# Half of the inner units at a time for the first two token blocks, with weight conversion at half the pace

## The chip, the cores and the metric

The kernel runs on one core of a Trainium2 chip. The metric is the device time of one execution in microseconds (us). Engines are called as the profile calls them: PE is TensorE's matmul, PEld its weight load, DVE is VectorE, ACT is ScalarE, POOL is GpSimd, and SP is SyncE, whose queue starts most DMAs.

## The reference

Three stages follow each other: a windowed attention, a routed mixture of eight experts, and a dense feed-forward with a squared ReLU. Only the last one is changed:

```python
def _moe2_ref(x, w_in, w_out):            # x [2176, 512], w_in [512, 2048], w_out [2048, 512]
    h = np.maximum(x @ w_in, 0.0)
    return (h * h @ w_out).astype(np.float32)
```

[...]

## The kernel before

**Precision.** Each matmul operand is split into a "high" float32r part and the "low" rest (`copy_hi` on ACT, line 65; `sub_lo` on DVE, line 68; `sub_lo_pool` on POOL, line 71), and each product is three matmuls: high by high, low by high, high by low.

**Token blocks and inner units.** The 17 tiles of 128 tokens make five blocks of 4, 4, 3, 3 and 3 tiles. The 2048 inner columns make 16 inner units of 128 (`FC2 = 16`), counted by `fc`. One *step* is `ff1(i, fc)` and then `ff2` of the step before. `ff1` runs 12 matmuls (lines 1105 to 1107) into a PSUM tile `fh`, ACT does Relu, Square and the high part (`ahi`), DVE the low part (`alo`). `ff2` runs 3 matmuls for each token tile (lines 1125 to 1127) and adds into PSUM tiles `fo` that stay open through all 16 steps of a block; only line 1127 reads `alo`. There are four `fo` buffers. After the 16th unit, `fo` is copied to an `os` tile (even token tiles on ACT, line 1133; odd ones on DVE, line 1131) and stored by a DMA of SP (line 1135).

**Inputs of a block.** `y_load` fetches a tile of the experts' output `yd` into `yin` (line 1082), `y_tile` transposes it on PE into `ytr` (line 1090) and splits it (`yhi`, `ylo`). `yin` and `os` share three buffers of the tag `io`.

**Weights.** The 32 weight units, 16 of `w_in` and 16 of `w_out` in turn, are loaded (`conv_load`, 512 KB each, three buffers), turned into float32 (`conv_value`: one instruction on ACT, line 717, five on DVE, lines 718 to 722) and split (`conv_split`: ACT, then POOL). A *tick* `k` of `conv` splits unit k - 2, converts unit k and starts the load of unit k + 2. All units then stay in SBUF. The first ten ticks lie among the experts (`on_take`, from chunk `CFROM = 12` on, one every `CSTEP = 5` chunks, at most `2 * NFE + 2` of them); the other 24 lie in the first block's steps, `RATE / 4` = 1.75 a step.

**Order.** Everything stands under a manual schedule: each engine, SP's queue too, runs its instructions in the order in which the program states them, and waits for what the next one needs.

Of the kernel before, what the change touches and what calls it, by code (L numbers as in the profile page):

```python
# [10 lines left out]
F32 = mybir.dt.float32  # L11
# [4 lines left out]
ALU = mybir.AluOpType  # L16
# [5 lines left out]
P = 128  # L22
NEG = -8e9
EXTRA = 3
# [5 lines left out]
def tile_attention_moe_ffn(  # L30
# [16 lines left out]
    nc = tc.nc  # L47
    B, H, S, D = q_l.shape
    SG = q_g.shape[2]
    NE, DM, FF = w1.shape  # L50
    FF2 = w_in.shape[1]
    ST = S + SG
    NTOK = B * ST
# [4 lines left out]
    FC2 = FF2 // P  # L58
# [16 lines left out]

    xd = dr.tile([NTOK, DM], F32, name="xd")
    yd = dr.tile([NTOK, DM], F32, name="yd")

# [1 line left out]
    ident = cp.tile([P, P], F32, name="ident")  # L80
    make_identity(nc, ident)
    mask = cp.tile([P, 3, KW], F32, name="mask")
# [10 lines left out]
    ths = cp.tile([P, MAXOV, NE], F32, name="ths")  # L93
    jrow = cp.tile([P, MAXOV], F32, name="jrow")

    # routing state
    rank = cp.tile([P, NTILE], F32, name="rank")
    ohs = cp.tile([P, NTILE, NE], BF16, name="ohs")
    val = cp.tile([P, NTILE, 4], F32R, name="val")
# [48 lines left out]
        g.memset(slot, 0.0)  # L148
        g.memset(ohsum, 0.0)

# [1 line left out]
    early = ctx.enter_context(ExitStack())  # L152
    wp = early.enter_context(tc.tile_pool(name="wp", bufs=1))
    LEADV = 5
    NRAW, NHL = 8, 6
    LOOK = NHL - 2
    NFE = 4
    RATE = 7
    CSTEP = 5
    CFROM = 12  # L160
    n_split = [0]

    def load_chunk(kind, p, c):
        """four rows of 128 of w1, or as many pairs of row blocks of w2"""
        raw = wp.tile([P, 1024], F32, tag="raw", bufs=NRAW, name="raw")
        e = pass_expert[p]
        w = w1 if kind == 1 else w2
        src = w[e:e + 1] if isinstance(e, int) else w[ds(e, 1)]
        if kind == 1:
            nc.sync.dma_start(out=raw, in_=src[:, c * P:(c + 1) * P, :].rearrange("o p f -> p (o f)"))  # L170
        else:
            r = c * 2 * P
            nc.sync.dma_start(
                out=raw.rearrange("p (k d) -> p k d", k=2),
                in_=src[:, r:r + 2 * P, :].rearrange("o (k p) d -> p (o k) d", p=P),
            )
        return raw
# [8 lines left out]
            sub_lo(lo, raw, hi)  # L186
        return hi, lo

    # an expert per pass: the first and the last by number, the others in an order found on the chip
    NX = NE  # L190
    pass_expert = {0: 0, 1: NE - 1}
    segs = [(1, 0)]
# [33 lines left out]
        on_take(i)  # L226
        return chunks.pop((kind, p, c))

    # =================== attention ===================
    att = ctx.enter_context(ExitStack())  # L230
    ap_ = att.enter_context(tc.tile_pool(name="ap", bufs=1))
    ps = att.enter_context(tc.tile_pool(name="ps", bufs=1, space=PSUM))
# [238 lines left out]
    cur = [0]  # L471

    def route(c, x):
        """gate, expert, rank within the expert and slot of the 128 tokens of tile c"""
        z = {}

        def s1():
# [88 lines left out]
            later.append((i0 + d_, f_, c, n_))  # L566
        later.sort(key=lambda p: p[0])

    # order of the attention's units
    units = []  # L570
    for b in range(B):
        for t in range(NT):
# [35 lines left out]
    with tc.manual_schedule():  # L608
# [61 lines left out]
            do_later()  # L670
        dv(len(micro))

        # =================== slots of the experts ===================
        att.close()
        fe = ctx.enter_context(tc.tile_pool(name="fe", bufs=1, side="right", reuse_waits="tile"))
        cv = ctx.enter_context(tc.tile_pool(name="cv", bufs=1, side="right", reuse_waits="tile"))
# [2 lines left out]
        mps = mo.enter_context(tc.tile_pool(name="mps", bufs=1, space=PSUM, reuse_waits="tile"))  # L679
        NHS, NHH = 4, 4  # L680

# [1 line left out]
        wpool = [fe]  # L683
        wff = {}
        craw, cval = {}, {}
# [47 lines left out]
            wff[u] = (hi, lo)  # L733

        def conv(ticks):
            """the first steps of the conversion: unit k - 2 split, unit k's value, unit k + 2 loading"""
            while n_conv[0] < min(ticks, NU + 2):
                k = n_conv[0]
                if k >= 2:
                    conv_split(k - 2)  # L740
                if k < NU:
                    conv_value(k)
                if k + 2 < NU:
                    conv_load(k + 2)
                n_conv[0] += 1
# [1 line left out]
        conv_[0] = conv  # L747

        def slot_indices(ids_, n, nm):
            """token + 1 (0: empty) -> rows to gather (empty: row 0) and to scatter (empty: beyond)"""  # L750
            gi = mp.tile([P, n], I32, name="gi" + nm)
            si = mp.tile([P, n], I32, name="si" + nm)
            em = mp.tile([P, n], F32, name="em" + nm)
            nc.vector.tensor_scalar(out=gi, in0=ids_, scalar1=-1.0, scalar2=0.0, op0=ALU.add, op1=ALU.max)
            nc.vector.tensor_scalar(out=em, in0=ids_, scalar1=0.0, scalar2=8192.0, op0=ALU.is_equal, op1=ALU.mult)
            nc.vector.scalar_tensor_tensor(out=si, in0=ids_, scalar=-1.0, in1=em, op0=ALU.add, op1=ALU.add)
            return gi, si
# [20 lines left out]
        gather_pass(0)  # L778
        gather_pass(1)

        # the experts between the first and the last, those with more than 128 tokens first: the
        # first EXTRA passes take two tiles; the general path takes what is left
        ND = NE - 2
        dd = slice(1, 1 + ND)
        tot = mps.tile([P, 512], F32, tag="tr", bufs=2, name="tot")
# [22 lines left out]
        nc.vector.tensor_copy(eji[:, ND:ND + 1], c1[:, 0:1])  # L808

        def all_bases():  # L810
            """first key and expert of every tile beyond the first of an expert, level by level"""
            lev = mp.tile([P, 2, MAXOV], F32, name="lev")
            nc.vector.tensor_reduce(out=lev[:, 0, :], in_=ov, op=ALU.add, axis=AX.X)
            fl = mp.tile([P, MAXOV, NE], F32, name="fl")
# [20 lines left out]
            return kb, kbi  # L835

        def all_keys():
            """rank + 4096 * expert + 1 of every routed token, 0 of the others"""
            key = mp.tile([P, NTILE], F32, name="key")
            kw = mp.tile([P, NTILE, NE], F32, name="kw")  # L840
            nc.vector.tensor_tensor(out=kw, in0=ohs, in1=ecol.unsqueeze(1).to_broadcast([P, NTILE, NE]), op=ALU.mult)
            nc.vector.tensor_reduce(out=key, in_=kw, op=ALU.add, axis=AX.X)
            nc.vector.tensor_tensor(out=key, in0=key, in1=rank, op=ALU.add)
            return key

        def any_slots(base, key):
            """slots of the tile whose first key is base"""
            acc = mps.tile([P, 512], F32, tag="tr", bufs=2, name="acc")
            kr = mp.tile([P, NTILE], F32, tag="kr", bufs=1, name="kr")
            nc.vector.tensor_scalar(out=kr, in0=key, scalar1=base, scalar2=-1.0, op0=ALU.subtract, op1=ALU.add)  # L850
            for c in range(NTILE):
                mt = mp.tile([P, P], F32R, tag="mt2", bufs=2, name="mt2")
                nc.vector.tensor_scalar(out=mt, in0=iota[:, 0:P], scalar1=kr[:, c:c + 1], scalar2=None, op0=ALU.is_equal)
                nc.tensor.matmul(acc[:, 0:4], mt, val[:, c, :], start=(c == 0), stop=(c == NTILE - 1))
            sl = mp.tile([P, 4], F32, tag="sl", bufs=1, name="sl")
            nc.vector.tensor_copy(sl, acc[:, 0:4])
            nc.vector.tensor_tensor(out=sl[:, 1:2], in0=sl[:, 1:2], in1=sl[:, 2:3], op=ALU.add)
            g_, s_ = slot_indices(sl[:, 0:1], 1, "g")
            return g_, s_, sl[:, 1:2]

# [1 line left out]
        n_over = nc.values_load(eji[0:1, ND:ND + 1], min_val=0, max_val=MAXOV, skip_runtime_bounds_check_because="counted")  # L862
        with tc.If(n_over > 0):
            kb, kbi = all_bases()
# [41 lines left out]
                    bounds_check=NTOK - 1, oob_is_err=False,  # L906
                )

        # =================== experts ===================
        conv_load(0)  # L910
        conv_load(1)
        sel = mp.tile([P, ND, ND], F32, name="sel")
# [138 lines left out]
        mo.close()  # L1051
        early.close()

        # =================== squared-ReLU feed-forward ===================
        fp = ctx.enter_context(tc.tile_pool(name="fp", bufs=1, reuse_waits="tile"))
        fps = ctx.enter_context(tc.tile_pool(name="fps", bufs=1, space=PSUM))
        wpool[0] = fp
# [35 lines left out]
            copy_hi(hi[:, :, c], mv)  # L1093
            sub_lo(lo[:, :, c], mv, hi[:, :, c])

        acts, outs = {}, {}

        def ff1(i, fc):
            n = sizes[i] * P
# [14 lines left out]
            sub_lo(lo[:, 0:n], r[:, 0:n], hi[:, 0:n])  # L1114
            acts[i, fc] = (hi, lo)

        def ff2(i, fc):
            hi, lo = acts.pop((i, fc))
            whi, wlo = wff[2 * fc + 1]
            if fc == 0:  # L1120
                outs[i] = [fps.tile([P, 512], F32, tag="fo", bufs=4, name="fo") for _ in range(sizes[i])]
            for j in range(sizes[i]):
                c = slice(j * P, (j + 1) * P)
                o = outs[i][j]
                nc.tensor.matmul(o, hi[:, c], whi, start=(fc == 0), stop=False)  # L1125
                nc.tensor.matmul(o, hi[:, c], wlo, start=False, stop=False)  # L1126
                nc.tensor.matmul(o, lo[:, c], whi, start=False, stop=(fc == FC2 - 1))  # L1127
                if fc == FC2 - 1:
                    a = fp.tile([P, DM], F32, tag="io", bufs=3, name="os")
                    if j % 2:  # L1130
                        nc.vector.tensor_copy(a, o)
                    else:
                        nc.scalar.copy(a, o)
                    r0 = (starts[i] + j) * P
                    nc.sync.dma_start(out=out[r0:r0 + P, :], in_=a)

        y_block(0)
        for j in range(3):
# [3 lines left out]
            if j == 0:  # L1142
                y_load(0, 3)
        prev = None
        for i in range(nb):
            for fc in range(FC2):
                ff1(i, fc)
                if i == 0:
                    conv(2 * NFE + 2 + RATE * (2 * fc + 1) // 8)
                if prev is not None:  # L1150
                    ff2(*prev)
                prev = (i, fc)
                if FC2 - 7 <= fc < FC2 - 3:
                    y_load(i + 1, fc - FC2 + 7)
                if i == 0:
                    conv(2 * NFE + 2 + RATE * (fc + 1) // 4)
                if i + 1 < nb:
                    if fc == FC2 - 5:
                        y_block(i + 1)
                    if FC2 - 5 <= fc < FC2 - 5 + sizes[i + 1]:  # L1160
                        y_tile(i + 1, fc - FC2 + 5)
        ff2(*prev)


# [26 lines left out]
```

## Time and profile before

| What | Value |
|---|---|
| Timed runs | median 846.65 us of 3 (845.98 to 846.96) |
| The profiled execution's own time (its span, first to last instruction) | 847.4 us |
| PE busy | 773.1 us, 91% |
| DVE busy | 438.4 us, 52% |
| ACT busy | 405.0 us, 48% |
| POOL busy | 164.0 us, 19% |
| HBM read and written | 74.21 MB and 16.25 MB |
| First `ff1` matmul of block 0, of block 1, of block 2 | 438.30, 547.56, 636.77 us |

The span is that of one profiled execution, on the slowest (here the only) core. The page gives nothing outside the span. A busy share is an average over the whole span, so the stretch that the change touches is read by itself.

### The profile page before, as it was taken

Reading aid. Unit: us, or ns where it says so; the run is one execution under the profiler, and the core shown is the slowest. Engines: PE = TensorE matmul, PEld = TensorE weight load, DVE = VectorE, ACT = ScalarE, POOL = GpSimd, SP = SyncE. Lnnn points to the kernel's source line nnn. Section 1 sums busy time; section 2 is a strip of 40 time slices with the busy share of each in tenths; the row PEclk is TensorE's granted clock in tenths of the full one; section 3 lists DMA queues with packets and bytes.
Section 4 is the critical chain, followed back from the end, with each engine's and each line's share of the span. In section 5 each row is a group of like instructions: output and inputs, shape, how many; then the busy total and the mean of one; then the engine's idle time right before and its main releaser. Section 6 shows DMA issues by size and latency. Waiting matters only on the chain.

```text
span 847.4 us, 12121 instructions
## 1 busy us (share of the span) xinstructions
PE 773.1 (91%) x4337; PEld 673.3 (79%) x4337; DVE 438.4 (52%) x1103; ACT 405.0 (48%) x863; POOL 164.0 (19%) x169
## 2 busy tenths in 40 slices
PE   7999999999938978796869878999999999999998
PEld 6998989989836968585647666788889999999997
DVE  5667656665544898898819999411111121111111
ACT  5666646545305764758116556333343344344333
POOL 4013200000013564748204344100000000000000
PEclk9999999999858999899869999999999999999999
DMA  9868954331126877777123445020002002000001
GB/s 178 203 161 189 239 136 99 98 84 51 50 70 212 264 228 249 241 276 258 37 87 92 132 129 169 1 87 1 1 1 87 1 1 75 1 1 38 1 1 38
DMA packets 103071, 90.35 MB, mean 107 GB/s; under 512 B 70594, under 2 KB 78786, under 8 KB 103008
## 3 DMA queue, kind: packets, MB, share of 16 engines
q1 hardware_dynamic: 101248, 84.71, 34.7%
q0 software_dynamic: 1760, 4.84, 1.7%
q8 instruction: 35, 0.57, 0.3%
q14 instruction: 28, 0.23, 0.1%
HBM read 74.21 MB, written 16.25 MB: 107 GB/s over the span
## 4 chain that ended last, share of the span: by engine, by line
PE 38%; DVE 9%; issue 2%; DMA 1%; ACT 0%; SPq 0%; POOLq 0%
PE fo L1127 6%; PE fh L1105 6%; PE fo L1126 6%; PE fh L1106 6%; PE fh L1107 6%; PE fo L1125 6%; DVE tb L719 2%; DVE tb L721 2%; DVE tb L720 2%; DVE alo L68 1%; DVE tb L722 1%; DVE ta L718 1%; PE ytr L1090 1%; DMA yin<-yd 1%; DMA yd<-y,six 0%
## 5 line engine op out<-in xcount | busy, mean ns | idle before, releaser
L68 DVE TENSOR_TENSOR alo<-fr,ahi 128x384 fp32r<-128x384 f32 (+1 forms) x80 | 48.8, 610 | 247.8 <-ACT ahi L65 247.8
L1109 ACT ACTIVATE fr<-fh 128x384 f32<-128x384 f32 (+1 forms) x80 | 42.7, 533 | 179.9 <-PE fh L1107 179.9
L1127 PE MATMUL fo<-whio,alo 128*128 128x512 f32 x272 | 108.6, 399 | 15.5 <-DVE alo L68 15.5
L1105 PE MATMUL fh<-yhi,whii 128*128 128x384 f32 (+1 forms) x320 | 117.1, 366 | 0.7 <-ACT yhi L65 0.7
L1106 PE MATMUL fh<-ylo,whii 128*128 128x384 f32 (+1 forms) x320 | 115.7, 362 | 0.0
L1107 PE MATMUL fh<-yhi,wloi 128*128 128x384 f32 (+1 forms) x320 | 115.6, 361 | 0.0
L1126 PE MATMUL fo<-wloo,ahi 128*128 128x512 f32 x272 | 107.7, 396 | 0.0
L1125 PE MATMUL fo<-whio,ahi 128*128 128x512 f32 x272 | 107.0, 394 | 0.0
L360 ACT ACTIVATE pbuf<-sw,min 128x224 f32<-128x224 f32 x128 | 60.7, 476 | 60.3 <-DVE min L355 48.8
L71 POOL TENSOR_TENSOR wlo<-raw,whi 128x1024 fp32r<-128x1024 f32 x28 | 70.2, 2511 | 70.7 <-ACT whi L65 67.9
L65 ACT ACTIVATE whi<-raw 128x1024 fp32r<-128x1024 f32 x64 | 65.5, 1058 | 27.1 <-PE o L1030 10.4
L1127 PEld LDWEIGHTS fo<-whio,alo 128*128 128x128 f32 x272 | 51.5, 189 | 30.6 <-DVE alo L68 19.5
L1105 PEld LDWEIGHTS fh<-yhi,whii 128*128 128x128 f32 x320 | 60.6, 190 | 8.1 <-ACT yhi L65 1.1
L1106 PEld LDWEIGHTS fh<-ylo,whii 128*128 128x128 f32 x320 | 60.7, 190 | 7.5 <-DVE ylo L68 0.4
L344 PE MATMUL s<-kt,qbuf 128*128 128x224 f32 x256 | 64.4, 375 | 1.0 <-ACT qbuf L332 0.7
L1107 PEld LDWEIGHTS fh<-yhi,wloi 128*128 128x128 f32 x320 | 60.6, 189 | 5.4
L68 DVE TENSOR_TENSOR wlo<-raw,whi 128x1024 fp32r<-128x1024 f32 x36 | 57.0, 1609 | 13.2 <-ACT whi L65 13.0
L1126 PEld LDWEIGHTS fo<-wloo,ahi 128*128 128x128 f32 x272 | 51.4, 189 | 9.9
L355 DVE CUSTOM_DVE_ANT_0 sw<-s,mask 128x224 f32<-128x224 f32 x128 | 48.2, 385 | 20.9 <-PE s L344 17.1
L1125 PEld LDWEIGHTS fo<-whio,ahi 128*128 128x128 f32 x272 | 51.4, 189 | 9.3
L429 PE MATMUL av<-vedge,pts 96*128 96x64 f32 x256 | 50.7, 281 | 0.0
L428 PE MATMUL av<-vmain,pts 128*128 128x64 f32 x256 | 50.3, 279 | 0.4 <-ACT pts L393 0.4
(209 smaller groups left out, 1526.1 us busy)
## 6 DMA issues: line engine op xcount, KB each, us to landing
raw<-in_moe_w SPq DMA_DIRECT2D x64, 512.0 KB, 4.9
wraw<-in_moe_w_in SPq DMA_DIRECT2D x16, 512.0 KB, 3.8
wraw<-in_moe_w_out SPq DMA_DIRECT2D x16, 512.0 KB, 3.5
yin<-yd SPq DMA_DIRECT2D x17, 256.0 KB, 3.0
out<-os SPq DMA_DIRECT2D x17, 256.0 KB, 2.0
kin<-in_k_l SPq DMA_DIRECT2D x16, 256.0 KB, 4.1
qin<-in_q_l SPq DMA_DIRECT2D x16, 256.0 KB, 4.7
vmain<-in_v_l SPq DMA_DIRECT2D x16, 256.0 KB, 4.7
```

The source lines that it names most:

```text
L65: nc.scalar.activation(dst, src, AF.Copy)
L68: nc.vector.tensor_tensor(out=dst, in0=src, in1=hi.bitcast(F32), op=ALU.subtract)
L71: nc.gpsimd.tensor_tensor(out=dst, in0=src, in1=hi.bitcast(F32), op=ALU.subtract)
L344: nc.tensor.matmul(s[j][:, 0:KW], qt[b, t][:, i, j, :], kt[b, t][:, i, :], start=True, stop=True)
L360: nc.scalar.activation(pb[:, j, 0:KW], w, AF.Exp, bias=mins[:, h:h + 1], scale=-1.0, accum_out=sums[:, h:h + 1])
L429: nc.tensor.matmul(o[:, h, :], a[0:3 * SG, j, 1, :], v_edge[b, t][:, h, :], start=False, stop=True)
L1105: nc.tensor.matmul(h[:, 0:n], whi[:, ks], yhi[:, k, :], start=(k == 0), stop=False)
L1106: nc.tensor.matmul(h[:, 0:n], whi[:, ks], ylo[:, k, :], start=False, stop=False)
L1107: nc.tensor.matmul(h[:, 0:n], wlo[:, ks], yhi[:, k, :], start=False, stop=(k == KC - 1))
L1125: nc.tensor.matmul(o, hi[:, c], whi, start=(fc == 0), stop=False)
L1126: nc.tensor.matmul(o, hi[:, c], wlo, start=False, stop=False)
L1127: nc.tensor.matmul(o, lo[:, c], whi, start=False, stop=(fc == FC2 - 1))
```

## The change

Three things change. (1) Blocks 0 and 1 are each done in two *turns* of eight inner units: block 0 first half, block 1 first half, block 0 second half, block 1 second half; the other blocks keep one turn of 16. The sums of a first half are copied out of `fo` and stored in a new DRAM tensor `zd`. In the last step of a second half they are loaded again (`part_load`, tiles `pin` of the tag `io`) and added to `fo` by DVE, in place of the copy to `os`. (2) `conv` runs one tick a step instead of 1.75, through the turns of both blocks. (3) `NFE` goes from 4 to 5: two more ticks come before the feed-forward, one in the last expert pass and one right after it, and two more weight units lie in the pool `fe`. Comments are removed too.

```diff
-    NFE = 4
-    RATE = 7
+    NFE = 5
+    CRATE = 4
...
+        HF = FC2 // 2
+        turns = [(0, 0, HF), (1, 0, HF), (0, HF, FC2), (1, HF, FC2)] + [(i, 0, FC2) for i in range(2, nb)]
+
+        def part_load(i, j):
+            r0 = (starts[i] + j) * P
+            a = fp.tile([P, DM], F32, tag="io", bufs=3, name="pin")
+            nc.sync.dma_start(out=a, in_=zd[r0:r0 + P, :])
+            parts[i, j] = a
...
-        def ff2(i, fc):
+        def ff2(i, fc, first, last):
...
+            if last and fc == FC2 - 1 and i < 2:
+                part_load(i, 0)
             for j in range(sizes[i]):
...
-                if fc == FC2 - 1:
-                    a = fp.tile([P, DM], F32, tag="io", bufs=3, name="os")
-                    if j % 2:
-                        nc.vector.tensor_copy(a, o)
+                if last:
+                    r0 = (starts[i] + j) * P
+                    if fc == FC2 - 1 and i < 2:
+                        if j + 1 < sizes[i]:
+                            part_load(i, j + 1)
+                        a = parts.pop((i, j))
+                        nc.vector.tensor_tensor(out=a, in0=o, in1=a, op=ALU.add)
                     else:
-                        nc.scalar.copy(a, o)
-                    r0 = (starts[i] + j) * P
-                    nc.sync.dma_start(out=out[r0:r0 + P, :], in_=a)
+                        a = fp.tile([P, DM], F32, tag="io", bufs=3, name="os")
+                        if j % 2:
+                            nc.vector.tensor_copy(a, o)
+                        else:
+                            nc.scalar.copy(a, o)
+                    nc.sync.dma_start(out=(out if fc == FC2 - 1 else zd)[r0:r0 + P, :], in_=a)
...
-        for i in range(nb):
-            for fc in range(FC2):
+        n_step = 0
+        made = 1
+        for i, f0, f1 in turns:
+            for fc in range(f0, f1):
                 ff1(i, fc)
-                if i == 0:
-                    conv(2 * NFE + 2 + RATE * (2 * fc + 1) // 8)
+                n_step += 1
+                conv(2 * NFE + 2 + CRATE * n_step // 4 - 1)
                 if prev is not None:
                     ff2(*prev)
-                prev = (i, fc)
-                if FC2 - 7 <= fc < FC2 - 3:
-                    y_load(i + 1, fc - FC2 + 7)
-                if i == 0:
-                    conv(2 * NFE + 2 + RATE * (fc + 1) // 4)
...
+                prev = (i, fc, fc == f0, fc == f1 - 1)
+                k = fc - f1
+
+                nx = made if made < nb and (made < 2 or f1 == FC2 and i == made - 1) else nb
+                if -7 <= k < -3:
+                    y_load(nx, k + 7)
+                conv(2 * NFE + 2 + CRATE * n_step // 4)
+                if nx < nb:
+                    if k == -5:
+                        y_block(nx)
+                    if -5 <= k < -5 + sizes[nx]:
+                        y_tile(nx, k + 5)
+                    if k == -1:
+                        made += 1
```

## Rows read from the trace of the kernel before

**Rows 1.** The page: DVE's busy tenths in 40 slices of the span.
```profile
DVE  5667656665544898898819999411111121111111
```
**Rows 2.** Windows of block 0 and block 1: busy time of each engine, clock, DMA.
```profile
438.30:547.56 109.26, 93.79 (x389) 73.55 (x389) 91.75 (x131) 58.26 (x98) 36.77 (x24) 0.96 0.32 102
547.56:636.77 89.21, 89.21 (x397) 73.28 (x396) 14.45 (x22) 32.55 (x53) 0.00 (x0) 1.00 0.06 21
```
**Rows 3.** PE's waits from 425 us to the end: total, times, longest.
```profile
PE fo L1127 <- DVE alo L68: 15.5, 9, 2.2
PE ytr L1090 <- DMA yin<-yd: 6.9, 2, 6.6
```
**Rows 4.** Groups of DVE instructions in block 0: busy us, mean ns, idle before.
```profile
L719 DVE TENSOR_SCALAR tb<-tb 128x512 f32<-128x512 f32 x22 | 22.5, 1021 | 0.0
...
L68 DVE TENSOR_TENSOR alo<-fr,ahi 128x512 fp32r<-128x512 f32 x16 | 11.0, 685 | 13.7 <-ACT ahi L65 13.7
...
L68 DVE TENSOR_TENSOR ylo<-ytr,yhi 128x512 fp32r<-128x512 f32 x5 | 3.4, 688 | 2.2 <-ACT yhi L65 2.2
```
**Rows 5.** Timeline of POOL and DVE in block 0: start, duration, instruction.
```profile
487.63 1.36 POOL L71 TENSOR_TENSOR wloo<-tb,whio 128x512 fp32r<-128x512 f32 x1 [1.75 <-ACT whio L65]
...
487.75 1.53 DVE L719 TENSOR_SCALAR tb<-tb 128x512 f32<-128x512 f32 x1
...
491.44 0.42 DVE L719 TENSOR_SCALAR tb<-tb 128x512 f32<-128x512 f32 x1
```
**Rows 6.** Timeline of PE in block 0, two of the nine waits.
```profile
467.54 0.50 PE L1127 MATMUL fo<-whio,alo 128*128 128x512 f32 x1 [2.05 <-DVE alo L68]
467.87 0.39 PE L1125 MATMUL fo<-whio,ahi 128*128 128x512 f32 x1
...
531.70 0.50 PE L1127 MATMUL fo<-whio,alo 128*128 128x512 f32 x1 [2.21 <-DVE alo L68]
...
535.69 0.60 PE L1090 MATMUL ytr<-ident,yin 128*128 128x128 f32 x4
```
**Rows 7.** Timeline of PE in block 1: first matmuls of four steps.
```profile
553.12 0.39 PE L1105 MATMUL fh<-yhi,whii 128*128 128x512 f32 x1
...
558.74 0.40 PE L1105 MATMUL fh<-yhi,whii 128*128 128x512 f32 x1
...
580.93 0.39 PE L1105 MATMUL fh<-yhi,whii 128*128 128x512 f32 x1
...
586.37 0.39 PE L1105 MATMUL fh<-yhi,whii 128*128 128x512 f32 x1
```
**Rows 8.** Timeline where block 0 ends and where block 1 ends.
```profile
552.98 3.22 SPq L1135 DMA_DIRECT2D out<-os  x4
...
553.12 0.68 DVE L1131 COPY os<-fo 128x512 f32<-128x512 f32 x1
...
555.92 0.40 PE L1125 MATMUL fo<-whio,ahi 128*128 128x512 f32 x1
...
641.21 0.68 DVE L1131 COPY os<-fo 128x512 f32<-128x512 f32 x1
...
643.79 0.39 PE L1125 MATMUL fo<-whio,ahi 128*128 128x512 f32 x1
...
645.62 0.56 DVE L68 TENSOR_TENSOR alo<-fr,ahi 128x384 fp32r<-128x384 f32 x1 [1.49 <-ACT ahi L65]
```
**Rows 9.** Issue to landing of the loads of yin, then the stores of os.
```profile
DMA to landing us min/median/max: 2.6/3.0/5.3
...
DMA to landing us min/median/max: 2.0/2.0/2.7
```
**Rows 10.** Where the experts end: DVE, POOL, and durations (min/median/max) of scatters.
```profile
426.04 0.75 DVE L1033 SCALAR_TENSOR_TENSOR y<-o,xs,xg 128x512 f32<-128x512 f32 x1 [4.89 <-PE o L1030]
...
427.07 0.97 POOL L1034 DMA_INDIRECT yd<-y,six  x1 [3.49 <-DVE y L1033]
...
L1034 POOL DMA_INDIRECT yd<-y,six x9: 966/1022/1212, 330.4 to 427.1; - x9
```

More of the change, by code (lines that the diff above doesn't have):

```diff
@@ L77, in tile_attention_moe_ffn @@
     yd = dr.tile([NTOK, DM], F32, name="yd")
+    zd = dr.tile([NTOK, DM], F32, name="zd")
     ident = cp.tile([P, P], F32, name="ident")
@@ L1094, in y_tile @@
             sub_lo(lo[:, :, c], mv, hi[:, :, c])
-        acts, outs = {}, {}
+        acts, outs, parts = {}, {}, {}
+        HF = FC2 // 2
[5 more added lines that the diff above has]
+            parts[i, j] = a
         def ff1(i, fc):
@@ L1115, in ff1 @@
             acts[i, fc] = (hi, lo)
-        def ff2(i, fc):
+        def ff2(i, fc, first, last):
             hi, lo = acts.pop((i, fc))
             whi, wlo = wff[2 * fc + 1]
-            if fc == 0:
+            if first:
                 outs[i] = [fps.tile([P, 512], F32, tag="fo", bufs=4, name="fo") for _ in range(sizes[i])]
+            if last and fc == FC2 - 1 and i < 2:
+                part_load(i, 0)
             for j in range(sizes[i]):
@@ L1124, in ff2 @@
                 o = outs[i][j]
-                nc.tensor.matmul(o, hi[:, c], whi, start=(fc == 0), stop=False)
+                nc.tensor.matmul(o, hi[:, c], whi, start=first, stop=False)
                 nc.tensor.matmul(o, hi[:, c], wlo, start=False, stop=False)
-                nc.tensor.matmul(o, lo[:, c], whi, start=False, stop=(fc == FC2 - 1))
-                if fc == FC2 - 1:
-                    a = fp.tile([P, DM], F32, tag="io", bufs=3, name="os")
-                    if j % 2:
-                        nc.vector.tensor_copy(a, o)
-                    else:
-                        nc.scalar.copy(a, o)
-                    r0 = (starts[i] + j) * P
-                    nc.sync.dma_start(out=out[r0:r0 + P, :], in_=a)
+                nc.tensor.matmul(o, lo[:, c], whi, start=False, stop=last)
+                if last:
[5 more added lines that the diff above has]
+                        nc.vector.tensor_tensor(out=a, in0=o, in1=a, op=ALU.add)
+                    else:
+                        a = fp.tile([P, DM], F32, tag="io", bufs=3, name="os")
[4 more added lines that the diff above has]
+                    nc.sync.dma_start(out=(out if fc == FC2 - 1 else zd)[r0:r0 + P, :], in_=a)
         y_block(0)
@@ L1144, in tile_attention_moe_ffn @@
         prev = None
-        for i in range(nb):
-            for fc in range(FC2):
+        n_step = 0
+        made = 1
+        for i, f0, f1 in turns:
+            for fc in range(f0, f1):
                 ff1(i, fc)
-                if i == 0:
-                    conv(2 * NFE + 2 + RATE * (2 * fc + 1) // 8)
+                n_step += 1
+                conv(2 * NFE + 2 + CRATE * n_step // 4 - 1)
                 if prev is not None:
                     ff2(*prev)
-                prev = (i, fc)
-                if FC2 - 7 <= fc < FC2 - 3:
-                    y_load(i + 1, fc - FC2 + 7)
-                if i == 0:
-                    conv(2 * NFE + 2 + RATE * (fc + 1) // 4)
[L1157 to L1161, printed above, removed]
+                prev = (i, fc, fc == f0, fc == f1 - 1)
[11 more added lines that the diff above has]
+                        made += 1
         ff2(*prev)
```

## The prediction

> **What bounds the kernel now.** I read the page's slices first, then the windows of two blocks, then PE's waits, and the timelines last. PE is busy for 91% of the span, so the first question is where the other 9% lies and what ends it. In the slices [rows 1] the reader is to see that DVE, after one slice of 1 tenth, is at 9 tenths for four slices (each is 847.4 / 40 = 21.2 us; the four run from 445 to 530 us) and soon after at 1 tenth for the rest: that is the weight conversion. The windows [rows 2] put block 0 beside block 1, which has nearly the same matmuls. Block 0 takes 109.26 us, with 93.79 of PE and 91.75 of DVE; block 1 takes 89.21 us, all of it PE. The waits [rows 3] say what fills the difference: nine times PE stands before line 1127 for `alo`, 15.5 us in all and never over 2.2 us. After 425 us PE has almost no other wait, but for 6.9 us on the first `yin`. From block 1 on PE is the bound by itself, and nothing that the change does to other engines can help there. So the only thing to be won is inside block 0.
>
> Why is `alo` late? Take from DVE's 91.75 us [rows 2] the 11.0 us of `alo` and the 3.4 us of `ylo` [rows 4]; 77.35 us are left for 22 conversions, 3.5 us each. A full step of PE takes 558.74 - 553.12 = 5.62 us [rows 7]. At 1.75 ticks a step DVE needs 1.75 x 3.5 + 0.69 = 6.8 us for each 5.62 us. DVE is the bound of block 0, by 1.2 us a step on average, and as ticks come in twos and ones, the lateness shows at about two steps of three.
>
> **What the change removes.** At one tick a step DVE needs 3.5 + 0.69 = 4.2 us, and 4.9 us in the four steps that also split a `ylo`, in which PE itself has four transposes more to do. Both are under 5.62, so the nine waits go. That gives back three sums. First, 15.5 us of waits [rows 3]. Second, the matmul after a wait holds PE for 467.87 - 467.54 = 0.33 us where the normal spacing is 5.62 / 24 = 0.234: 0.1 for eight waits, 0.8 us. Third, after the wait at 531.70 the ten matmuls up to 535.69 take 3.99 us [rows 6] where ten spacings take 2.34: 1.65 us. Over block 0 the granted clock is 0.96 of full speed against 1.00 in block 1 [rows 2]: for part of it PE ran at 1.2 instead of 2.4 GHz, and one such part is this one, begun right after a wait of 2.21 us. The other part is block 0's start after the idle stretch on `yin`; that one stays. Sum: 15.5 + 0.8 + 1.65 = 18.0 us.
>
> Are weights then ready in time? After step n, units up to n + 9 are split; step 8 wants units 14 and 13, step 17 wants unit 16. They are always two or more steps ahead. The same ticks now reach into block 1's first half and five steps of block 0's second half. DVE is idle there today: 14.45 us busy of 89.21 [rows 2]. If that cover failed, a step would lose what DVE is over 5.62.
>
> **What it adds, first halves.** Two more ends of a block with four `os` copies and four stores each. At such an end today PE goes straight on at 555.92 [rows 8], with no wait of PE on `fo` in [rows 3]: the copies finish while `ff1` runs. Now a tick (3.5 us) stands behind them on DVE. The third copy instruction of DVE's part waits for the first store to land, 552.98 + 2.0 [rows 9], and is over at 555.7; the tick then ends at 559.2 and the next `alo` at 559.9. It is wanted by the third matmul of `ff2`, at 555.92 + 5.62 + 0.47 = 562.0. Cost taken: 0; it becomes a cost once DVE is over 2.1 us later than this.
>
> **What it adds, second halves.** Four adds on DVE take the place of two copies there and two on ACT; an add of PSUM and SBUF into SBUF has a close row in `ylo`, 0.688 us [rows 4]. The price is the order. On SP's queue `pin0` and `pin1` stand ahead of the first store and are loaded long before, but `pin2` stands behind the store of sum 0, and `pin3` needs the buffer of `pin0`, so its store must have landed. Lay this on the end of block 0 [rows 8]: DVE's first add runs from 553.12 to 553.81; the store starts at 553.85 and holds SP for 0.34 us; `pin2` starts at 554.19 and lands after 3.0 us [rows 9], at 557.2; add 2 ends at 557.9. The store of sum 0 lands after 2.0 us at 555.85; `pin3` starts at 555.95 and lands at 558.95; add 3 ends at 559.64. PE wants `fo` 2 at 555.92 + 6 x 0.234 = 557.33 and waits 0.57; it then wants `fo` 3 at 558.60 and waits 1.04. With 0.1 for each restart: 1.8 us. Behind add 3 stands the next `alo`, 560.3 at the end, wanted at 563.6 or later: hidden. The same on the end of block 1, where the next block has three tiles and `fo` 3 isn't wanted: first add from 641.21, `pin2` starts at 642.28 and lands at 645.28, add 2 ends at 645.97, wanted at 643.79 + 1.40 = 645.19: 0.8, with the restart 0.9 us. The `alo` that runs at 645.62 today then ends at 648.3, and is wanted after 649. Sum: 2.7 us. Bounds: with the shortest landing of 2.6 [rows 9] it is 1.9 us; with the longest of 5.3 each end loses 2.3 more, 7.3 us. I take the median's 2.7, as DMA is busy for 0.06 of block 1 [rows 2].
>
> **Steps themselves.** A step of block 1 takes 5.62 us early and 586.37 - 580.93 = 5.44 later [rows 7], with no wait in either; the longer ones lie where DMAs move. Conversion steps, with their 512 KB loads, rise from 24 / 1.75 = 14 to 22. If all eight more are of the longer kind, it costs 8 x 0.18 = 1.4 us; as loads come at half the pace, perhaps nothing. I take 0.7.
>
> **Two more ticks before the feed-forward.** The first falls into the last expert pass, where DVE has 4.89 us idle before 426.04 [rows 10] for its 3.5 us; the second comes behind the last scatter, in PE's wait of 6.6 us for the first `yin` [rows 3]. Their loads (`wraw`) start when older buffers come free, before the scatter's data moves. The cover is thin at one place: the last scatter's instruction on POOL at 427.07 (0.97 us) starts the chain that ends PE's wait, and DVE's conversion now runs beside it. Scatters take 0.966 to 1.212 us [rows 10]; the step to the longest is 0.25 us, and I take it. Below it: 0. Above it: if the first tick holds up the instruction at 426.04, about 1 us.
>
> That DVE and POOL get in each other's way is seen in [rows 5]: the same line 719 takes 0.42 us alone and 1.53 us when it starts behind POOL's 1.36 us, which it outlasts by 0.3. It is in the 3.5 us already. The Trainium skill, "SBUF — State Buffer", section "Who interferes with whom", says that POOL and some DVE instructions take one shared pair of SBUF ports as a whole, and that whichever starts second waits until the first is over; by that rule it is a lock and not a slowdown, and the rows here agree. The same rule speaks against this edit, since it lets DVE shut POOL out of writing a scatter's descriptors: by it the last scatter could be held for two such DVE instructions of 0.42 us, and the sum would be 0.6 us higher, an estimate from [rows 5] and that page.
>
> **The sum.** 847.4 - 18.0 + 2.7 + 0.7 + 0.25 = 833.05 us of span. The median of the timed runs, 846.65, is 0.75 below the profiled span, so the forecast for the timed median is 832.3 us, 1.7% faster.
>
> **Rivals.** (a) *No stall at the second halves* and quicker steps: if `pin2` and `pin3` don't hold up PE, the terms 2.7 and 0.7 fall away: 828.9. For it: PE's matmuls may lag a little where sums are read. Against it: the queue order above. (b) *The part sums are late*: landings of 5.3 us at both ends [rows 9] give 7.3 instead of 2.7: 836.9. For it: reads right behind writes of the same tensor group, and stores and loads of one queue mixed. A drop of PE's clock behind such a wait, 1.65 us once [rows 6], would land near here too. (c) *DVE stays late in some steps*: a slow instruction (1.1 us, [rows 5]) in each of the six steps that also hold a `ylo` or copies: +6.6, 838.9. Against it: the copy at 553.12 stands right behind an `alo` that is wanted only at 555.92 + 0.47 = 556.4, so there are some 3 us in hand. (d) *Slower*: DVE takes its instructions in order, so a late `pin2` or `pin3` holds the next `alo` and both `fo` buffers, and each us of lateness costs a us at each of two ends. To eat the 14.35 us that are left, landings must be 7.2 us over 3.0; at 10.2 us the change is even, above it slower. The longest landing seen is 5.3. (e) *No effect*, that is, DVE's lateness only moves to block 1: DVE would need over 5.62 us for a tick and an `alo` where it has needed 4.2; about 847.
>
> **How the numbers follow.** Forecast with its two small stalls (829.5 to 835): 0.68. Rival (a) 0.10, (b) 0.11, (c) 0.06, (d) 0.03, (e) 0.02. The range from 829 to 837 holds the forecast, most of (b) and part of (a). A measurement of this kernel tells about 0.2% (1.7 us) from no change. Faster: 0.68 + 0.10 + 0.11 + 0.06 = 0.95; same 0.02; slower 0.03.
>
> **What the profile after would show.** Right: no wait of line 1127 for `alo` in the first 24 steps; the two first-half turns pass with PE full and a granted clock of 1.00 after the first steps; DVE at 7 to 8 tenths over twice as many slices; PE waiting on a DVE add at two places only, about 1.6 and 0.8 us; the first `ff1` matmul of the feed-forward still near 438.3. Wrong: waits for `alo` that stay; a wait on `fo` where first halves end; a first `ff1` later than 439; or new low-clock stretches behind the adds.

## The result, and the profile after

The changed kernel takes 833.48 us (median of 4 runs, 830.68 to 835.96) against 846.5 us before: ratio 0.9845, 95% interval 0.9819 to 0.9871. A second time, with 6 runs (825.83 to 835.92), it took 830.34 us, ratio 0.9794 (0.9753 to 0.9835). The profiled execution has a span of 828.7 us and took 830.68 us, so 2 us lie outside the span. Each ratio, here and below, is to runs of the kernel before that were made beside them, with medians of 846.1 to 847.2 us. Lines of the changed kernel: `ff1` is at 1117 to 1119, `ff2` at 1139 to 1141, the add at 1148, the part loads at 1107, `conv_value` at 718 to 723.

The page's slices of the changed kernel (busy tenths of PE and DVE; compare [rows 1]):

```profile
PE   7999999999966979799559999999999999999998
DVE  5657766566543889798966777751122121111111
```

DVE's four full slices are gone; from the 21st on it works at 6 to 7 tenths for six slices. The 21st, 414 to 435 us, holds the two moved ticks; behind it the pace is 1 tick a step for 1.75, so a little over half and not half. The windows of the changed kernel, with borders at the first `ff1`, near the begin of the second halves, and at block 2:

```profile
435.39:526.05 90.66, 90.66 (x389) 73.32 (x390) 67.82 (x99) 50.15 (x86) 20.04 (x16) 0.97 0.33 104
526.05:616.92 90.87, 88.91 (x397) 72.91 (x396) 33.56 (x50) 38.24 (x64) 9.24 (x7) 1.00 0.20 65
616.92:828.70 211.78, 207.28 (x1045) 186.57 (x1043) 35.46 (x62) 80.91 (x156) 0.00 (x0) 1.00 0.08 27
```

In the first window PE has no idle time at all, with DVE busy for 67.82 us of 90.66; before, block 0 had 93.79 of 109.26 [rows 2]. Blocks 0 and 1 together take 616.92 - 435.39 = 181.5 us, and 636.77 - 438.30 = 198.5 before. PE's waits from 415 us on, which answer to [rows 3]:

```profile
PE ytr L1091 <- DMA yin<-yd: 7.2, 2, 6.9
PE fo L1139 <- DVE pin L1148: 2.7, 3, 1.1
```

No wait for `alo` is left. The new wait is for DVE's adds, three times. This is the end of block 0's second half (timeline of SP, DVE and PE):

```profile
575.59 0.34 SPq L1155 DMA_DIRECT2D out<-pin  x1
575.98 0.42 SPq L1107 DMA_DIRECT2D pin<-zd  x1
...
577.61 0.32 SPq L1107 DMA_DIRECT2D pin<-zd  x1
...
579.21 0.69 DVE L1148 TENSOR_TENSOR pin<-fo,pin 128x512 f32<-128x512 f32 x1 [3.05 <-issue]
...
579.95 0.50 PE L1139 MATMUL fo<-whio,ahi 128*128 128x512 f32 x1 [0.88 <-DVE pin L1148]
...
581.26 0.69 DVE L1148 TENSOR_TENSOR pin<-fo,pin 128x512 f32<-128x512 f32 x1 [1.36 <-DMA pin<-zd]
...
582.01 0.50 PE L1139 MATMUL fo<-whio,ahi 128*128 128x512 f32 x1 [1.08 <-DVE pin L1148]
```

The third part load goes out at 575.98, right behind the first store, and the fourth at 577.61, 2.0 us after that store began, when its buffer is free. Adds 2 and 3 start as these loads land, 3.1 and 3.5 us after their issue, and PE waits for each of them.

**One measure for all kernels.** Call the stretch from the first `ff1` matmul to the end of the span the feed-forward. The table gives it for every profiled execution, beside the median of the timed runs.

| Kernel | Median us | Ratio to before (95%) | First `ff1` | Span | Feed-forward |
|---|---|---|---|---|---|
| before | 846.5 | | 438.30 | 847.4 | 409.1 |
| changed | 833.48 | 0.9845 (0.9819 to 0.9871) | 435.39 | 828.7 | 393.3 |
| again | 830.34 | 0.9794 (0.9753 to 0.9835) | 440.15 | 834.0 | 393.8 |
| split_alone | 850.44 | 1.0029 (1.0006 to 1.0052) | 435.22 | 848.4 | 413.2 |
| pace_alone | 833.3 | 0.9846 (0.9813 to 0.9878) | 431.22 | 827.1 | 395.9 |
| pins_early | 827.19 | 0.9762 (0.9732 to 0.9791) | 434.38 | 824.0 | 389.6 |
| ticks_back | 832.59 | 0.9821 (0.9792 to 0.985) | 435.28 | 831.8 | 396.5 |
| four_ops | 835.97 | 0.9872 (0.9844 to 0.99) | 432.82 | 833.1 | 400.3 |
| fe_aligned | 824.97 | 0.974 (0.9715 to 0.9765) | 435.37 | 824.7 | 389.3 |
| all_aligned | 826.65 | 0.9751 (0.9724 to 0.9779) | 436.01 | 823.3 | 387.3 |
| split_on_dve | 831.88 | 0.9832 (0.9804 to 0.9861) | 429.83 | 826.5 | 396.7 |
| pace_and_dve | 821.85 | 0.9705 (0.9672 to 0.9738) | 428.63 | 819.7 | 391.1 |
| fe_low | 827.58 | 0.9778 (0.9747 to 0.9809) | 435.21 | 825.6 | 390.4 |
| halves_and_dve | 820.06 | 0.9697 (0.9672 to 0.9721) | 433.46 | 822.8 | 389.3 |

### The profile page after: what moved, and what is told of

It reads as the page before. It is cut to its first block, busy times and chain, and to the rows that moved or that the text cites. A ratio compares the mean times of both kernels' runs of the same rounds, so it can differ in the third digit from the quotient of the medians.

```text
span 828.7 us, 12169 instructions
## 1 busy us (share of the span) xinstructions
PE 768.3 (93%) x4337; PEld 671.3 (81%) x4337; DVE 442.4 (53%) x1111; ACT 404.1 (49%) x863; POOL 161.0 (19%) x169
```

## The experiments

### again: where the spread comes from

The changed kernel, unchanged.

> The changed kernel itself, once more, for a second trace and for the spread of its four runs (830.68 to 835.96). My theory: the feed-forward takes 393 us from its first ff1 matmul to the end of the span in every execution, as in the first trace (435.39 to 828.7), and the spread of 5 us lies in the expert stage ahead of it, whose PE waits on splits come and go in each execution; then the first ff1 starts anywhere from 435 to 441. Rival: the spread comes from the loads of the part sums or from waits in the first half turns; then the feed-forward itself differs by several us between the traces and the first ff1 stays near 435. Median by either: 831 to 836, ratio 0.981 to 0.988.

The two traces differ in the first `ff1` (rows of the changed kernel's first and second trace):

```profile
435.39 0.79 PE L1117 MATMUL fh<-yhi,whii 128*128 128x512 f32 x1 [0.69 <-ACT yhi L65]
...
440.15 0.80 PE L1117 MATMUL fh<-yhi,whii 128*128 128x512 f32 x1 [0.69 <-ACT yhi L65]
```

From there the stage takes 393.3 and 393.8 us. So, as far as two traces tell, most of the spread of the timed runs lies ahead of the feed-forward, and its length is the sharper measure of an edit in it: 15.8 and 15.3 us less than before. It has a spread of its own: its first step, at a granted clock of 0.50 to 1.00, takes 3.4 to 5.6 us in the fourteen traces, so a difference of a us or two between two traces has to be found in their steps. The median, 830.34, and the lowest timed run, 825.83, are under what I had said.

### split_alone: the halves without the slower pace

```diff
-    NFE = 5
+    NFE = 4
-    CRATE = 4
+    CRATE = 7
```

> The blocks in halves as in the changed kernel, but the conversion at the old pace of 1.75 ticks a step and from the old starting point. My theory, DVE's pace is what holds PE and the halves by themselves only cost: the waits for alo stay at nine or so and 15 us, spread over 14 steps, and the two ends with part sums add their waits (2.7 us and restarts); 847 to 851, ratio 1.000 to 1.006. Rival, the halves themselves bring the gain: 832 to 835, no waits for alo.

```profile
PE fo L1141 <- DVE alo L68: 8.4, 6, 2.2
...
PE fh L1118 <- DVE ylo L68: 5.0, 1, 5.0
PE fo L1139 <- DVE pin L1148: 2.7, 3, 1.0
```

PE's waits: `alo` and `ylo` together 13.4 us, the adds 2.7. The feed-forward is 4.1 us longer than before and the time 0.3% longer. The halves by themselves only cost. The waits for `alo` are fewer and smaller than the 15 us that I had expected, and one for `ylo` makes up for most of it. What I had not seen: with the ticks packed into 14 steps, block 1's `ylo` stood behind them on DVE, and PE waited 5.0 us at the first step of block 1.

### pace_alone: the slower pace without the halves

```diff
-    NFE = 4
+    NFE = 5
...
-                    conv(2 * NFE + 2 + RATE * (2 * fc + 1) // 8)
+                    conv(2 * NFE + 2 + 23 * (2 * fc + 1) // 32)
...
-                    conv(2 * NFE + 2 + RATE * (fc + 1) // 4)
+                    conv(2 * NFE + 2 + 23 * (fc + 1) // 16)
```

> The kernel before, blocks whole and nothing in DRAM, but with the two ticks moved ahead of the feed-forward and the rest spread over all 16 steps of block 0 (23 ticks in 16 steps, the least at which every weight unit is split in time). DVE then needs 1.44 x 3.5 + 0.69 + 0.17 = 5.9 us a step for PE's 5.4 to 5.6 us with 0.1 for transposes. My theory, only DVE's total in block 0 counts: about 0.2 to 0.4 us late a step, 3 to 6 us of waits in the last two thirds of the block, and no stall on part sums (3.6 us in the changed kernel): 831 to 836, within 0.3% of the changed kernel. Rival, the halves are needed because two ticks in one step hold alo back whatever the mean: waits of 2 us stay in the seven steps with two ticks, 838 to 842.

```profile
PE fo L1127 <- DVE alo L68: 2.7, 4, 0.9
PE fh L1107 <- POOL wloi L71: 1.1, 1, 1.1
```

The waits for `alo` fall from 15.5 to 2.7 us and the feed-forward by 13.2 us, with no halves. Five sixths of the gain come from the pace, moved ticks included; the waits are a little under the 3 to 6 us that I had expected. The 1.1 us is the price of the late end: the last units are split just when they are wanted.

### pins_early: the two stalls taken away

Four buffers for `io`, and all four part loads ahead of the first store.

```diff
-                part_load(i, 0)
+                for j in range(sizes[i]):
+                    part_load(i, j)
...
-                        if j + 1 < sizes[i]:
-                            part_load(i, j + 1)
```

> The changed kernel with four io buffers in place of three and with all four part sums of a block loaded ahead of its first store. My theory, the order on SP's queue and the shared buffer make the two stalls: the three waits of PE for DVE's adds (2.7 us, with restarts 3.6) go, and it is 3 to 4 us faster than the changed kernel, ratio to the kernel before 0.977 to 0.984. Rival, DVE's adds are late for themselves (behind alo, or by four of them in a row): the waits stay within 1 us of what they were.

PE's only waits from 420 us on:

```profile
PE ytr L1091 <- DMA yin<-yd: 7.9, 2, 7.0
PE fh L1117 <- ACT yhi L65: 0.7, 1, 0.7
```

The waits for the adds are gone and the feed-forward is 389.6 us, 3.7 less than the changed kernel's first trace. So the order on SP's queue and the shared buffer made the stalls, not DVE's adds; which of the two counts for how much was not tried.

### ticks_back: the two ticks in the steps again

```diff
-    NFE = 5
+    NFE = 4
```

> The changed kernel with NFE at 4, so the two ticks that it moved ahead of the feed-forward are back in the steps: 24 ticks in 24 steps. My theory, they were hidden there but for a quarter of a microsecond of the last scatter: the scatter's instruction falls from 1.25 to 0.97 us, PE's wait for the first yin from 6.9 to 6.6 us, and the feed-forward from its first ff1 matmul to the end stays at 393 to 394 us, as DVE still has the room. The time is that of the changed kernel within the spread of the expert stage. Rival, the two ticks matter: alo is late again somewhere in the first 24 steps and the feed-forward grows by 2 us or more.

The scatter did fall, from 1.25 to 0.97 us (rows of the changed kernel, then of this one):

```profile
423.91 1.25 POOL L1035 DMA_INDIRECT yd<-y,six  x1 [2.17 <-DVE y L1034]
...
424.13 0.97 POOL L1035 DMA_INDIRECT yd<-y,six  x1 [3.48 <-DVE y L1034]
```

But the feed-forward is 396.5 us, 3.2 longer, so I was wrong that it stays; the rival had the size right and not the cause, as `alo` is never late:

```profile
PE fo L1139 <- DVE pin L1148: 2.9, 3, 1.1
PE fh L1119 <- POOL wloi L71: 0.9, 2, 0.6
```

With two ticks fewer ahead, PE waits twice, for the low part of units that POOL splits just in time; these two steps are 0.5 and 1.1 us longer than in the changed kernel. Another 1.4 us has another cause. The step after the first two stalls on the adds has no wait in it, but a lower granted clock (windows of that step in the changed kernel, then here):

```profile
582.80:588.26 5.46, 5.46 (x25) 4.50 (x24) 0.55 (x1) 1.86 (x3) 0.00 (x0) 1.00 0.59 195
...
584.46:591.36 6.90, 6.90 (x26) 5.54 (x24) 0.57 (x1) 1.86 (x3) 0.00 (x0) 0.78 0.44 146
```

The clock is 0.78 instead of 1.00: for part of the step PE ran at 1.2 GHz, right behind two waits of 0.99 and 1.10 us. The prediction had named such a drop in rival (b). Behind the same stalls in three other traces (the changed kernel's two and `split_alone`) this step takes 5.46 to 5.48 us; what decides it stays open. So the two moved ticks bought a lead of the weights that is worth 1.6 us of the 3.2, and not all of it.

### four_ops: one DVE instruction of a conversion left out

```diff
-            nc.vector.tensor_scalar(out=tbf, in0=tbf, scalar1=EXP_LO, scalar2=EXP_HI, op0=ALU.max, op1=ALU.min)
```

> The kernel before with one of the five DVE instructions of a conversion left out, the one that holds a weight's exponent within its limits (line 719; what it leaves out changes only weights outside those limits). Blocks whole, 1.75 ticks a step. That instruction has 1.02 of the 3.5 us. My theory, DVE's need for a step alone makes alo late: 1.75 x 2.5 + 0.69 = 5.1 us is under PE's 5.4 to 5.6, so most of the nine waits go, at most 3 us stay, and the feed-forward falls from 409 to 391 to 394 us: 829 to 834 in all, with no halves and nothing in DRAM. Rival, the two ticks in one step or POOL's splits hold alo back: waits of 8 us or more stay, 838 to 844.

The weights arrive as 64-bit floats, and this instruction limits their exponents on the way to 32 bits. The waits for `alo`, then DVE and POOL in a step of two ticks:

```profile
PE fo L1126 <- DVE alo L68: 8.6, 7, 1.5
```

```profile
460.71 1.36 POOL L71 TENSOR_TENSOR wloi<-tb,whii 128x512 fp32r<-128x512 f32 x1 [1.76 <-ACT whii L65]
...
461.01 1.61 DVE L719 SCALAR_TENSOR_TENSOR tb<-tb,ta 128x512 int32<-128x512 int32 x1
...
464.97 1.41 DVE L720 TENSOR_SCALAR tb<-tb 128x512 int32<-128x512 int32 x1
```

The waits stay at 8.6 us, as the rival had it, and the feed-forward at 400.3 lies between the two theories: my number for a tick was wrong. The 0.42 us of work went, but not the wait of about 1 us behind POOL: another instruction now takes it. Line 719 here is what was line 720, and takes 1.61 us behind POOL where it needs 0.69 us alone. A tick costs 3.05 us by DVE's busy time (82.57 us from 432.82 to 533.18, less 12.1 of `alo` and 3.4 of `ylo`, over 22), so 1.75 ticks and an `alo` still need 6.0 us a step, and PE is still held. With that number the theory of DVE's need fits.

### split_on_dve: POOL taken out of the weights' conversion

```diff
-            sub_lo_pool(lo, w, hi)
+            sub_lo(lo, w, hi)
```

> The kernel before, but the low parts of the feed-forward's weights are made by DVE (line 68) instead of POOL; all else as it was, 1.75 ticks a step in block 0. With one of the five instructions left out a tick fell only from 3.5 to 3.05 us, since the 1.1 us of waiting for POOL went to the next instruction. Theory, POOL's 1.4 us shut DVE out of SBUF and cost it 1.1 us a tick: without POOL a tick is 0.42 + 0.42 + 0.69 + 0.43 + 0.69 and 0.69 for the new instruction, less some overlap, 3.2 to 3.3 us; a step of two ticks falls from 7.85 to 7.2 to 7.4 us, the waits from 15.5 to 9 to 12 us, and the feed-forward from 409 to 401 to 406 us, though DVE does more work. Rival, the slow instructions have another cause: a tick grows by 0.6 to 0.7, a two-tick step to 9 us and the feed-forward to 416 to 420 us.

```profile
PE fo L1127 <- DVE alo L68: 6.0, 6, 1.3
```

```profile
L719 DVE TENSOR_SCALAR tb<-tb 128x512 f32<-128x512 f32 x22 | 9.2, 420 | 0.0
...
L68 DVE TENSOR_TENSOR wloi<-tb,whii 128x512 fp32r<-128x512 f32 x12 | 8.2, 685 | 0.0
```

Line 719 is at 0.42 us everywhere (before, it took 0.42 or about 1.5 us, 1.02 on average [rows 4]), and DVE, with one instruction more for each unit, is busy for less: 82.06 us in block 0 against 91.75 [rows 2]. A tick costs (82.06 - 11.0 - 3.4) / 22 = 3.1 us, a step of two ticks 7.0. The waits fall to 6.0 us and the feed-forward to 396.7, both further than I had said, on the old pace and with whole blocks: this one word gives 12.4 of the changed kernel's 15.8 us.

### pace_and_dve: the even pace and DVE's splits, whole blocks

Both edits: `pace_alone` and `split_on_dve`.

> The kernel with whole blocks and the conversion spread over 16 steps (the earlier run with the pace alone, 395.9 us of feed-forward), with DVE making the weights' low parts as well. DVE's need is 1.44 x 3.25 + 0.69 + 0.17 = 5.5 us a step, about PE's. Theory: the waits for alo, 2.7 us there, nearly go, and the wait of PE for POOL's low part (1.1 us) goes: feed-forward 391 to 394 us, level with the changed kernel's 393.3 without any halves. Rival, halves are needed: waits of 3 us or more stay, 396 or above.

```profile
PE fh L1107 <- DVE wloi L68: 1.4, 1, 1.4
```

That is PE's only wait left in the blocks' steps. Feed-forward 391.1 us, less than the changed kernel's, with nothing in DRAM; 821.85 us in all. The expectation missed one thing: PE still waits 1.4 us for a low part, now DVE's, at the end of block 0.

### halves_and_dve: halves, early part sums and DVE's splits

Both edits: `pins_early` and `split_on_dve`.

> Halves as in the changed kernel, part sums loaded early on four buffers, and the weights' low parts made by DVE instead of POOL. Theory: DVE's need is 3.25 + 0.69 = 3.9 us a step, far under PE's, so the feed-forward is that of the early part sums, 389.6 us, or 1 to 2 us under the whole blocks with DVE (391.1); the first ff1 comes at 428 to 431, as in the two kernels with DVE's splits; 819 to 822 in all, ratio to the kernel before 0.966 to 0.974, level with the whole blocks within what a measurement tells. Rival, the early start of those two was chance: the first ff1 lies at 434 to 440 as in the kernels that split on POOL, and the time is 825 to 831.

820.06 us, the fastest median here; its interval (0.9672 to 0.9721) and that of `pace_and_dve` (0.9672 to 0.9738) nearly coincide, so the halves can't be told from the whole blocks by time once POOL is out; the feed-forward is 1.7 us shorter, about what the late low part at the end of block 0 costs `pace_and_dve`. The start is not settled by the trace, with the first `ff1` at 433.46, between the two expectations; taking 2 us and 389.3 off the median leaves 428.8, as in `pace_and_dve`.

### fe_aligned, all_aligned, fe_low: why are early steps longer?

`fe_aligned` puts 32 bytes above the pool `fe`, `all_aligned` 32 bytes more into the experts' pool, and `fe_low` swaps `fe` and `cv`, all on top of `pins_early`.

```diff
+        pd = ctx.enter_context(tc.tile_pool(name="pd", bufs=1, side="right", reuse_waits="tile"))
+        pad = pd.tile([P, 8], F32, name="pad")
+        nc.vector.memset(pad, 0.0)
```

> The kernel with the early part sums, with a tile of 32 bytes put above the pool fe, so that its weight units start at multiples of 64 bytes instead of 32 past one. In all traces so far the steps whose units lie in fe (the first four, or five with NFE at 5) take 5.6 us in blocks of four tiles, and the later ones 5.44, also where no DMA and no conversion runs. Theory, the place of the operands in SBUF: the early steps fall to 5.44 in every block and the feed-forward from 389.6 to 387 to 388 us. Rival, it is the time since the block began, or DMAs and conversions: the early steps stay at 5.6 and the feed-forward at 389.6.

> The same with 32 bytes more in the experts' pool too, so that the split activations there (xhi, xlo, hhi, hlo) start at multiples of 64 bytes. Theory of the place in SBUF: the experts' matmuls of 512 columns go from 0.233 to 0.227 us apart; as the expert stage is held by splits and loads for much of its time, perhaps 2 us of 180. Rival: the spacing stays at 0.233 and so does the stage, within its spread of 4 us.

> The kernel with the early part sums, with the pools fe and cv in the other order, so that fe lies 20 KB lower in SBUF and the conversion's buffers at the top. Theory, the matmuls whose weights lie in the upper part of SBUF are 3% further apart: the steps of the lowest units fall to 5.44 us while those of the highest stay at 5.6, and the feed-forward loses up to 2 us of 389.6. Rival, it is the pool's own history (written early, by the same instructions): all five steps stay at 5.6.

None of them moved it: the early steps take 5.55 to 5.59 us in the first two and up to 5.62 in the third, and the experts' matmuls of 512 columns stay 0.233 us apart in `all_aligned`. The 387.3 us of `all_aligned` come from its first two steps, 8.96 us where the other kernels take 10.4 to 11.6: the granted clock is 1.00 in its first step, and 0.50 to 0.60 in the changed kernel's two traces, `fe_aligned`, `fe_low` and `pace_and_dve`. Three misses.

## Why the prediction was right, point by point

**DVE as the bound of block 0: shown.** `split_alone` keeps the pace and keeps 13.4 us of waits for `alo` and `ylo` where there were 15.5; `pace_alone` changes the pace and loses 12.8 of 15.5 us of them. In both DVE's need a step decides.

**The gain, 18.0 us: right in kind, 1.7 us too small.** Before, the nine steps of block 0 with a wait are together 19.7 us longer than the same steps of block 1, which have none. The waits are 15.5 of that, and the low clock behind the wait at 531.70 is 1.65, as I had it. The other 2.6 us lie around the nine waits, 0.23 to 0.34 at each, where I had taken 0.1 for eight of them. That term, 0.8 us, is the one that was mis-sized. The profile counts a wait from the end of the matmul ahead, and these matmuls overlap:

```profile
465.10 0.40 PE L1126 MATMUL fo<-wloo,ahi 128*128 128x512 f32 x1
467.54 0.50 PE L1127 MATMUL fo<-whio,alo 128*128 128x512 f32 x1 [2.05 <-DVE alo L68]
```

At the usual spacing the second would have started 0.23 us after the first, at 465.33. So 2.21 us are lost ahead of it and not 2.05, and the 0.1 that I had seen behind it come on top.

**The steps, 0.7 us: measured 0.2, and the reason was wrong.** Blocks 0 and 1 are 16.9 us shorter, and this holds the first two waits on the adds: their step takes 7.98 us where its neighbours take 5.44. So 19.5 us went, 0.2 less than the 19.7. I had said that the longer steps lie where DMAs move. In the changed kernel steps take 5.44 us from the 15th on, while conversion and loads still run (the last load of weights is issued at 536.70); what the longer ones share are the units of the pool `fe`, of which there are now two more. First matmuls of the 13th and 14th step (5.60 us apart, units in `fe`), then of the 17th and 18th (5.44 us, units elsewhere, a tick on DVE beside them):

```profile
503.83 0.40 PE L1117 MATMUL fh<-yhi,whii 128*128 128x512 f32 x1
...
509.43 0.39 PE L1117 MATMUL fh<-yhi,whii 128*128 128x512 f32 x1
...
525.87 0.39 PE L1117 MATMUL fh<-yhi,whii 128*128 128x512 f32 x1
...
531.31 0.39 PE L1117 MATMUL fh<-yhi,whii 128*128 128x512 f32 x1
```

**The two stalls, 2.7 us: place and cause right, size 3.6.** The waits themselves are 2.7 us by the profile (0.88, 1.08 and 0.79), where I had 2.4 (0.57, 1.04 and 0.8); each also costs 0.25 to 0.3 us around it and not 0.1, for the reason just given. The loads that PE waits on land in 3.1, 3.5 and 2.9 us, where I had taken 3.0. `pins_early` shows the cause.

**The two moved ticks, 0.25 us: right for the scatter.** Its instruction takes 0.97 us in the traces with NFE at 4 and 1.25 to 1.26 with NFE at 5 (1.16 to 1.17 where DVE splits), and PE's wait for the first `yin` grew from 6.6 us before to 6.9. Their worth was missed: I counted weights as ready by steps of the program, while POOL's split ends later than its place in the order says; without the two ticks PE waits 0.9 us, and the steps in question are 1.6 us longer.

**First halves' ends at nothing: right.** No wait on `fo` stands there, though DVE waited 2.6 us in all for stores.

**The base and the number.** Stepping 0.75 us down from the span to the median sets the change, 14.35 us, against the median; that the profiled execution was itself some 3 us longer than the median's (847.4 and 2 us outside, against 846.5) did no harm by this. The medians measured are 13.0 and 16.3 us under those of the kernel before, and the feed-forward is 15.8 and 15.3 us shorter. The forecast of 832.3 us came out near both medians, 833.48 and 830.34, as the errors of its terms partly cancel: 1.7 us more of gain, 0.9 more of stalls, 0.5 less in the steps. The two medians of the one kernel are 3.1 us apart, more than the 1.7 us that I had said a measurement tells.

**The signs.** The first halves' turns pass with PE full, and the adds hold PE at two places only, for 1.96 and 0.79 us, as forecast; DVE is at 6 to 7 tenths over six slices, a little less than the 7 to 8 that I had named. One sign of being wrong did appear: the first `ff1` in the second trace is at 440.15, later than 439. It could not tell anything, since the stage ahead moves it by several us between executions of one kernel. No low clock stands behind the adds in the changed kernel's two traces.

**POOL and DVE.** The prediction read the 1.1 us behind POOL as a part of the tick that can't be helped. `four_ops` shows that it goes to whatever DVE instruction is next, and `split_on_dve` that taking it out is worth 12.4 of the 19.7 us. The Trainium skill, "SBUF — State Buffer", section "Who interferes with whom", says that a VectorE instruction with two SBUF inputs also contends with a GpSimd instruction that reads SBUF; the 1.61 us of line 719 in `four_ops` agrees. By the same section of the Trainium skill the prediction had estimated a scatter held by two DVE instructions of 0.42 us; the trace shows it held for 0.28 us, less than one.

## What to carry to other kernels

Before splitting work so that a slow engine can keep pace, look at single instructions of that engine for two durations of the same form: here 0.42 and 1.53 us said that POOL's help cost DVE more than the work that it took over (1.1 us against 0.69). When a load must follow stores of the same queue, issue it ahead of them and give it its own buffer, or the store's wait becomes the load's. Where a stage ahead varies by several us between executions, compare lengths of the stage that was edited and not whole times, and read the granted clock of steps that are long without a wait. And count what a wait costs from the start that was due, not from the end of the matmul ahead: here that is 0.16 us more for each.

## What was not expected of the hardware

Apart from steps with transposes in them or just ahead, steps of four tiles whose weight units lie in the pool `fe` take 5.6 us and the others 5.44, with the granted clock at 1.00 in both: with NFE at 4 the fifth unit's step is the first shorter one (5.52), with 5 the sixth's (5.54). Start at a multiple of 64 bytes, a place 20 KB lower, and DMA activity don't explain it; what does stays open. The experts' stage may also end earlier in kernels whose feed-forward weights are split by DVE: the median less 2 us and the feed-forward gives 428.8 us for `pace_and_dve` and `halves_and_dve`, and 434 to 436 for `pins_early` and `ticks_back`. Their first ticks lie in that stage. But `split_on_dve`, which splits on DVE too, gives 433.2, and single executions of the changed kernel give 430 to 441, so this is not shown, and POOL's hold on DVE was not tried there by itself.
